# Sums of states as the moving side, and gate weights turned on VectorE, in the head of an attention and expert kernel

## The chip, the cores and the metric

The kernel runs on one core of one Trainium2 chip. The metric is the device time of one execution in microseconds (us). Three executions of the kernel before took 437.92, 438.87 and 439.55 us; the median is 438.87. The profiled execution has a span of 434.3 us, and all times within the program are counted from the start of that span.

## What is computed

The first block is a cross attention between tokens x and states, for each of 8 batches and 8 heads, with 512 tokens, 32 states and a head width of 64:

```python
scores = scale * np.matmul(x, state.transpose(0, 1, 3, 2))
a = softmax(scores)
xread = np.matmul(a, state)          # tokens read states
a2 = softmax(scale * np.matmul(state, x.transpose(0, 1, 3, 2)))
sread = np.matmul(a2, x)             # states read tokens
rows = concatenate([xread, sread])   # (8 * 544 rows, 512 wide)
```

The second block routes each of these 4352 rows to one of 8 experts:

```python
logits = rows @ w_gate                       # 512 x 8
e = argmax(logits);  gate = softmax(logits)[e]
out = gate * (maximum(rows @ w1[e], 0) @ w2[e])   # w1: 512 x 1024, w2: 1024 x 512
```

All of it is float32.

## The kernel before, in words

The kernel takes the batches one after the other. For most batches nearly all token rows go to one and the same expert, so a batch is computed with the expert that most of its rows choose, and the rows that chose otherwise are treated apart at the end. Because a token row is a weighted mean of states, the kernel never forms it: it multiplies the states of the batch with w1 (a product called G, from PSUM tiles pG), and then G with the turned attention weights (aT) to get the hidden layer (PSUM tiles ph, SBUF tiles hT), and last with w2 (py, pX and other PSUM tiles).

**The order** of all instructions is written out by hand: each engine's wrapper `InOrder` (line 48, hence the L48 in nearly every row of the profile) keeps the program order on its engine. A wait at the head of an engine's queue holds all that is behind it. The scheduler adds the semaphores between engines.

**The head.** Batch 0 has a start of its own, `begin` (line 443). Before it, the program issues the first loads: `load_states(0, sp, act)` (line 111) puts the 32 state rows into partitions 0 to 31 of `st2[0]` with one DMA on SyncE's queue, and the same rows with the two halves of each head exchanged into partitions 32 to 63 with two DMAs on ScalarE's queue. Then ScalarE's queue issues the gate weights `wg4` (line 112), in which partition p holds rows 4p to 4p+3 of w_gate, and SyncE's queue the two halves of x of batch 0 (line 113). VectorE and GpSimd prepare constants meanwhile; VectorE ends this with a memset of `gst` (line 187), a tile of which only 8 of each 32 columns are written later.

`begin` first makes a guess of batch 0's expert, so that w1 can be fetched before attention is computed: the column sums of the states times w_gate. `keep_warm(n)` (line 543) issues n matmuls of the identity with itself into a PSUM tile that nobody reads (`idle`); they keep TensorE busy. A float32 matmul shows as two records in the profile. The sums are four matmuls (PSUM tile `pss`), whose stationary side is a strided piece of the states of 32 x 128 and whose moving side is one column of ones; VectorE copies them to `sums` (128 x 4), and four more matmuls (`prg`) multiply them with the columns of wg4. `most` (line 435) finds the number of the largest of 8 on VectorE (`c_m`, `c_cc`, `eb`), and `expert_of` (line 549) reads it into a register of SyncE, after which SyncE issues the two halves of that expert's w1, then x and states of batch 1, the gate weights in another order, w2, and batch 2.

In the meantime VectorE turns the states in blocks of 32 x 32 (`turn_states`, tile `stT`, of which ScalarE copies the lower partitions to the upper ones, and GpSimd makes the copies `stG` that pG uses) and then the first half of x (`turn_x`, tile `xt`). TensorE runs six warming matmuls and then the scores of batch 0 (PSUM tile `pc`), 64 matmuls of 32 x 32 x 128; the first half of them needs stT and the first half of x. Behind pc, VectorE and ScalarE compute the softmax in pieces (`sx`, `mx`, `sm`) and turn it to aT (tile `aTe`), and TensorE multiplies G with it.

Of the kernel before, what the change touches and what calls it, by code (L numbers as in the profile page):

```python
# [9 lines left out]
FP32 = mybir.dt.float32  # L10
# [3 lines left out]
ALU = mybir.AluOpType  # L14
AX = mybir.AxisListType
# [5 lines left out]
def kernel(  # L21
# [32 lines left out]
    pe, dve, act, gp, sp = (InOrder(e) for e in (nc.tensor, nc.vector, nc.scalar, nc.gpsimd, nc.sync))  # L54
# [4 lines left out]
    E = moe_w_gate.shape[1]  # L59
# [7 lines left out]
    NDC = DM // 128  # L67
# [21 lines left out]
    att = tc.alloc_tile_pool(name="att", bufs=1)  # L89
# [3 lines left out]
    def load_x(b, q):  # L93
        x_nat[b] = att.tile([128, H, NC, D], FP32, tag="x", bufs=3, name="x_nat")
        for h in (slice(0, 4), slice(4, 8)):
            q.dma_start(out=x_nat[b][:, h].rearrange("p h c d -> p h (c d)"),
                        in_=x[b, h].rearrange("h (p c) d -> p h (c d)", c=NC))

    st2 = {}

    def load_states(b, q0, q1):

        rows = state[b].rearrange("h n d -> n h d")
        to = st2[b] = att.tile([64, H, D], FP32, tag="st", bufs=3, name="st2")
        q0.dma_start(out=to[0:32], in_=rows)
        for u in range(2):
            q1.dma_start(out=to[32:64, :, ts(u, 32)], in_=rows[:, :, ts(1 - u, 32)])

    wg = const.tile([128, NDC, E], FP32)
    wg4 = att.tile([128, NDC, E], FP32, name="wg4")  # L110
    load_states(0, sp, act)
    act.dma_start(out=wg4[:], in_=moe_w_gate.rearrange("(p c) e -> p c e", c=NDC))
    load_x(0, sp)
    warm = const.tile([128, 1], FP32)
    dve.memset(warm[:], 0.0)
    act.activation(warm[:], warm[:], AF.Exp)
# [2 lines left out]
    ident = const.tile([128, 128], FP32)  # L119
# [12 lines left out]
    ones_f = att.tile([128, 1], FP32, name="ones_f")  # L132
# [51 lines left out]


    gst = att.tile([128, B, 2, 32], FP32, name="gst")
    dve.memset(gst[:], 0.0)


    blank = ffn.tile([128, XW], I32, tag="y", bufs=YB, name="blank")  # L190
    gp.memset(blank[:], 0)
    gp.memset(blank[:, DM + 1:DM + 2], FAR)

    soft, rows_of = {}, {}
    G = hT = None

    def bank(name):
        return ps_p.tile([128, 512], FP32, tag="p", name=name)
# [3 lines left out]
    def turn_x(b, xt, k):  # L202

        dve.transpose(xt[k][:].rearrange("p h c u t -> p (h c u t)"),
                      x_nat[b][:, ts(k, 4)].rearrange("p h c d -> p (h c d)"))

    def turn_states(b, copy):

        stT[b] = att.tile([128, H, 2, NS], FP32, tag="stT", bufs=2, name="stT")
        to = stT[b][:].rearrange("p h u n -> p (h u n)")  # L210
        dve.transpose(to[0:64], st2[b][:].rearrange("p h d -> p (h d)"))
        copy(to[64:128], to[0:64])
        for g in range(2):
            gp.tensor_copy(out=stG[ts(g, 64), b], in_=stT[b][:].rearrange("p (q g) u n -> p g u q n", g=2)[ts(g, 64), g, 0])
# [61 lines left out]
    def new_xt(b):  # L276

        return [(att, ffn)[b % 2].tile([128, 4, NC, 2, 32], FP32, tag=("xt0", "xt1", "Sa", "Sb")[2 * (b % 2) + k], name="xt")
                for k in range(2)]

    def new_sx():
        return att.tile([128, 4, NB, NS], FP32, tag="sx", bufs=2, name="sx")
# [152 lines left out]
    def most(b, pr):  # L435
        n = pr.shape[0]
        m = att.tile([n, 1], FP32, tag="c_m", bufs=2, name="c_m")
        dve.tensor_reduce(m[:], pr, AX.X, ALU.max)
        cc = att.tile([n, E], FP32, tag="c_cc", bufs=2, name="c_cc")
        dve.scalar_tensor_tensor(cc[:], pr, m[:], io8[0:n], ALU.is_ge, ALU.mult)  # L440
        dve.tensor_reduce(eb[0:n, b:b + 1], cc[:], AX.X, ALU.max)

    def begin():

        nonlocal G, hT

        keep_warm(3)
        ps = bank("pss")[:, 0:4]
        for q in range(4):
            pe.matmul(ps[:, q:q + 1], lhsT=st2[0][0:32].rearrange("n h d -> n (h d)").rearrange("n (p c) -> n c p", c=4)[:, q, :],  # L450
                      rhs=ones_f[0:32], start=True, stop=True, skip_group_check=True)
        sums = att.tile([128, 4], FP32, name="sums")
        dve.tensor_copy(out=sums[:], in_=ps)
        pr = bank("prg")[0:1, 0:E]
        for q in range(4):
            pe.matmul(pr, lhsT=sums[:, q:q + 1], rhs=wg4[:, q, :], start=(q == 0), stop=(q == 3), skip_group_check=True)
        most(0, pr)
        keep_warm(6)
        turn_states(0, act.copy)
        xt, sx = new_xt(0), new_sx()  # L460
        turn_x(0, xt, 0)
        e = expert_of(eb, 0)
        at_once(w1_parts(0, e, 2))
        load_x(1, sp)
        load_states(1, sp, sp)
        sp.dma_start(out=wg[:], in_=moe_w_gate.rearrange("(c p) e -> p c e", p=128))
        at_once(w2_parts(0, e))
        fetch_batch(2)
        turn_x(0, xt, 1)
        pc = new_pc()  # L470
        for qs in ((0, 1), (2, 3)):
            for g in range(2):
                scores(0, xt, pc, g, qs)
        one, two, half = slice(0, 1), slice(1, 2), slice(2, 4)
        soft[0] = (sx,)
        G, hT = new_G(), new_hT()
        turn_scores(pc, sx, 0)
        less_max(sx, one, dve)
        exponential(sx, one)
        states_w1(G, w1s[0], stG[:, 0], (0,), cut=2)  # L480
        turn_scores(pc, sx, 1)
        over_sum(sx, one, dve)
        turn_read(0, one)
        less_max(sx, two, dve)
        exponential(sx, two)
        keep_warm(5)
        near, far = range(NFC // 2), range(NFC // 2, NFC)
        up(G, aT[0], hT, one, fs=near)
        states_w1(G, w1s[0], stG[:, 0], (1,))
        turn_scores(pc, sx, 2)  # L490
        turn_scores(pc, sx, 3)
        over_sum(sx, two, dve)
        turn_read(0, two)
        up(G, aT[0], hT, two, fs=near)
        less_max(sx, half, dve)
        exponential(sx, half)
        over_sum(sx, half, dve)
        turn_read(0, half)
        for r in range(NR):
            sp.dma_start(out=ss_dram[ts(r, 128)], in_=blank[:])  # L500
        up(G, aT[0], hT, one, fs=far)
        up(G, aT[0], hT, two, fs=far)
        nm = write_max(pc)
        xt, sx = new_xt(1), new_sx()
        for k in range(2):
            turn_x(1, xt, k)
        turn_states(1, gp.tensor_copy)
        first_e = att.tile([1, 1], FP32, name="first_e")
        dve.tensor_copy(out=first_e[:], in_=eb[0:1, 0:1])

        def beside():
            nonlocal nm, pc
            soft[0] += write_weights(pc, nm)
            states_gates(0)
            yield
            states_gates(1)
            pc = new_pc()
            scores(1, xt, pc, 0)
            yield

            pr = bank("pre")[:, 0:1]
            pe.matmul(pr, lhsT=ones_f[0:1].to_broadcast([1, 128]), rhs=first_e[:], start=True, stop=True)
            scores(1, xt, pc, 1)
            dve.tensor_copy(out=eb[:, 0:1], in_=pr)
            for i in range(4):
                turn_scores(pc, sx, i)
            less_max(sx, ALL, dve)
            nm = write_max(pc)
            yield
            exps, gates = logits_x(0)  # L530
            turn_write(0)
            exponential(sx, ALL)
            soft[1] = (sx,) + write_weights(pc, nm)
            exps()
            early.append(stages(2))
            next(early[0])
            gates()
            over_sum(sx, ALL, dve)
            turn_read(1)
            yield  # L540
        up(G, aT[0], hT, half, beside())

    def keep_warm(n):

        idle = bank("idle")
        for _ in range(n):
            pe.matmul(idle[:, 0:128], lhsT=ident[:], rhs=ident[:], start=True, stop=True, skip_group_check=True)

    def expert_of(table, i, engines=(SP,)):
        _, (e,) = nc.values_load_multi_w_load_instructions(  # L550
            table[0:1, i:i + 1], engines=list(engines), min_val=0, max_val=E - 1,
            skip_runtime_bounds_check_because="the table holds experts' numbers")
        return e
# [16 lines left out]
    def at_once(parts):  # L570
        for p in parts:
            p()
# [616 lines left out]
    with tc.If(number(rest_i, B * S + NG) > 0, label="rest") as cmp:  # L1189
# [4 lines left out]
        with tc.If(number(left_i, B * S) > 0):  # L1194
# [18 lines left out]
            with tc.For_i(0, n_pairs, 1):  # L1213
# [14 lines left out]
                e = expert_of(px, 0)  # L1228
# [5 lines left out]
                             in_=at_dram[ds(bb, 1)].rearrange("o p s -> p (o s)"))  # L1234
# [61 lines left out]
```

## Time and profile before

| | busy us | share of the span |
|---|---|---|
| TensorE matmul (PE) | 425.9 | 98% |
| TensorE weight load (PEld) | 289.6 | 67% |
| VectorE (DVE) | 220.3 | 51% |
| GpSimd (POOL) | 153.3 | 35% |
| ScalarE (ACT) | 129.0 | 30% |

In the first 16 us the engines stand thus:

| start us | what |
|---|---|
| 0.84, 1.29, 1.79 | ScalarE's queue issues the two pieces of states and the gate weights |
| 0.87, 1.33 | SyncE's queue issues the state rows and the two halves of x |
| 1.47 to 3.12 | first warming matmuls |
| 3.34 to 5.33 | sums of the states |
| 6.29 to 6.64 | prg |
| 6.57 to 9.50 | second warming matmuls |
| 9.43 to 12.33 | scores pc |
| 13.27 to 14.48 | first half of pG |
| 16.14 | first products ph |

A row of the profile names the tile that is written and those that are read (out<-in), the shapes, the count, and in brackets the idle time of the engine just before and what ended it. PE is a matmul, PEld a load of its stationary side; an engine's name with a q is its queue, as where a DMA is issued. Busy time of an engine that works beside another costs nothing; what counts is the chain of waits, in which each piece of time is put down to the work that the next piece waited for.

### The profile page before, as it was taken

What the parts mean: (1) busy time and instruction counts of PE and PEld (TensorE: products, weight loads), DVE (VectorE), ACT (ScalarE), POOL (GpSimd) and SP (SyncE); (2) the same over time, 40 slices, a digit from 0 to 9 for tenths busy, and PEclk for the clock granted to TensorE, in tenths of its full rate; (3) what the DMA queues carried; (4) which work ended last, traced back from release to release, by engine and by line L of the source; (5) the groups of instructions that cost most, each with busy time, mean ns of one, the idle gap of its engine ahead of it and who ended that gap; (6) DMA issues with size and microseconds to landing.
All of it is one profiled execution on the core that took longest, in us unless ns stands there. A gap on an engine that the chain in (4) does not pass through costs nothing.

```text
span 434.3 us, 10177 instructions
## 1 busy us (share of the span) xinstructions
PE 425.9 (98%) x3927; PEld 289.6 (67%) x3927; DVE 220.3 (51%) x473; ACT 129.0 (30%) x297; POOL 153.3 (35%) x143
## 2 busy tenths in 40 slices
PE   7899999999999999999999999999999999999996
PEld 7676555555545558686668667776867685768665
DVE  5668966587686547434424251624442370527142
ACT  1455134552451532213221241013240242015100
POOL 2010231233222513473327424634335253644231
PEclk9999999999999999999999999999999999999999
DMA  5991559753685444999999699689947998875312
GB/s 144 342 344 41 188 191 307 225 211 122 206 307 171 157 172 129 293 341 390 384 386 395 220 342 384 250 279 397 386 151 239 406 379 281 312 260 200 97 36 73
DMA packets 64513, 110.04 MB, mean 253 GB/s; under 512 B 12943, under 2 KB 22415, under 8 KB 64464
## 3 DMA queue, kind: packets, MB, share of 16 engines
q1 hardware_dynamic: 60240, 99.99, 66.7%
q0 software_dynamic: 2240, 7.08, 4.3%
q10 hardware_dynamic: 1984, 2.31, 1.5%
q8 instruction: 32, 0.52, 0.5%
q14 instruction: 17, 0.14, 0.1%
HBM read 94.15 MB, written 14.95 MB: 251 GB/s over the span
## 4 chain that ended last, share of the span: by engine, by line
PE 95%; DVE 2%; DMA 1%; ACT 0%; issue 0%; ACTq 0%; POOL 0%; DVEq 0%
PE ph L48 23%; PE py L48 13%; PE pX L48 10%; PE pD L48 8%; PE pY L48 5%; PE pZ L48 5%; PE pgh L48 5%; PE pgy L48 5%; PE pW L48 5%; PE pc L48 4%; PE pG L48 3%; PE pw L48 2%; PE pt L48 2%; PE pE L48 2%; DMA wg<-in_moe_w_gate_dram 1%; PE pl L48 1%
## 5 line engine op out<-in xcount | busy, mean ns | idle before, releaser
L48 PE MATMUL py<-w2t,hT 128*128 128x512 f32 x128 | 59.1, 604 | 0.0
L48 DVE TENSOR_TENSOR hT<-ph,hT 128x512 f32<-128x512 f32 x50 | 34.6, 692 | 40.7 <-PE ph L48 40.7
L48 POOL TENSOR_TENSOR Ta<-w2t,Ta 128x1024 f32<-128x1024 f32 x12 | 30.6, 2549 | 46.6 <-PE pY L48 19.9
L48 PE MATMUL pX<-w2t,hT 128*128 128x256 f32 x192 | 43.7, 381 | 0.0
L48 PEld LDWEIGHTS py<-w2t,hT 128*128 128x128 f32 x128 | 23.0, 189 | 26.3 <-issue 25.3
L48 PEld LDWEIGHTS pX<-w2t,hT 128*128 128x128 f32 x192 | 36.2, 190 | 6.4 <-issue 1.7
L48 ACT ACTIVATE hT<-ph 128x512 f32<-128x512 f32 (+2 forms) x50 | 22.7, 462 | 40.1 <-PE ph L48 40.1
L48 PE MATMUL ph<-aTl,G 128*128 128x256 f32 (+1 forms) x112 | 33.8, 444 | 0.0
L48 DVE SCALAR_TENSOR_TENSOR yh<-pY,gw,yh 128x256 f32<-128x256 f32 x22 | 9.2, 478 | 44.3 <-PE pY L48 37.7
L48 PE MATMUL ph<-aTe,G 128*128 128x128 f32 (+2 forms) x128 | 30.4, 388 | 0.5 <-DVE aTe L48 0.4
L48 ACT ACTIVATE yh<-pX,gw 128x256 f32<-128x256 f32 x34 | 13.7, 474 | 52.6 <-PE pX L48 52.6
L48 POOL DMA_DIRECT2D out_dram<-yh x23 | 16.8, 730 | 34.3 <-DVE yh L48 17.7
L48 ACT ACTIVATE hT<-hT 128x512 f32<-128x512 f32 x30 | 18.9, 630 | 30.7 <-DVE hT L48 30.7
L48 PEld LDWEIGHTS ph<-aTl,G 128*128 128x128 f32 x112 | 20.6, 190 | 9.6 <-issue 7.7
L48 POOL TENSOR_TENSOR sx<-sx,mx 128x1024 f32<-128x1024 f32 x6 | 11.5, 1913 | 38.4 <-DVE mx L48 38.4
L48 PEld LDWEIGHTS ph<-aTe,G 128*128 128x128 f32 x128 | 18.8, 191 | 9.3 <-issue 6.5
L48 ACT COPY G<-pG 128x512 f32<-128x512 f32 (+1 forms) x34 | 17.1, 568 | 24.3 <-PE pG L48 24.3
L48 ACT COPY hT<-ph 128x512 f32<-128x512 f32 x10 | 5.9, 586 | 55.1 <-issue 43.1
L48 PE MATMUL pY<-Ta,Sa 128*128 128x256 f32 x96 | 22.2, 384 | 0.0
L48 PE MATMUL pZ<-Tb,Sb 128*128 128x256 f32 x96 | 22.1, 383 | 0.0
L48 PEld LDWEIGHTS pY<-Ta,Sa 128*128 128x128 f32 x96 | 17.8, 190 | 6.4 <-issue 3.4
L48 POOL TENSOR_TENSOR Tb<-w2t 128x1024 f32<-128x1024 f32 x6 | 14.2, 2370 | 22.2 <-issue 22.2
(184 smaller groups left out, 737.5 us busy)
## 6 DMA issues: line engine op xcount, KB each, us to landing
s<-in_moe_w_dram SPq DMA_DIRECT2D x192, 256.0 KB, 5.9
w2t<-in_moe_w_dram SPq DMA_DIRECT2D x32, 512.0 KB, 6.8
w1t<-in_moe_w_dram SPq DMA_DIRECT2D x28, 512.0 KB, 6.8
x_nat<-in_x_dram SPq DMA_DIRECT2D x16, 512.0 KB, 5.3
out_dram<-yh POOLq DMA_DIRECT2D x23, 256.0 KB, 5.2
at_dram<-aTl SPq DMA_DIRECT2D x6, 512.0 KB, 6.4
w1t<-in_moe_w_dram SPq DMA_DIRECT2D x2, 1024.0 KB, 5.1
out_dram<-y ACTq DMA_DIRECT2D x8, 256.0 KB, 5.6
```

The source lines that it names most:

```text
L48: ins = getattr(self.engine, name)(*args, **kw)
```

## The change

The guess of batch 0's expert is computed in another way. The states become the moving side of four matmuls against a 32 x 32 block of ones: the matmul of column group q gives the sums of columns 128q to 128q+127, repeated in 32 partitions. The gate weights are loaded first on ScalarE's queue, into a tile padded with zeros to 32 columns for each of the four rows of a partition, and VectorE turns that tile in blocks of 32 x 32, so that partition 32q+e holds the 128 weights of expert e for group q. VectorE multiplies the sums with them and adds over the 128 elements. Four matmuls against columns of the identity add the four groups and bring the eight logits into one partition. The purpose is a guess that needs less TensorE work before it and does not wait for the gate weights.

Besides, one of the first warming matmuls is dropped, the memset of gst moves from VectorE to GpSimd, and the first half of x is turned ahead of the states rather than behind them.

```diff
-    wg4 = att.tile([128, NDC, E], FP32, name="wg4")
+    wg4 = att.tile([128, NDC, 32], FP32, name="wg4")
+    act.dma_start(out=wg4[:, :, 0:E], in_=moe_w_gate.rearrange("(p c) e -> p c e", c=NDC))
     load_states(0, sp, act)
-    act.dma_start(out=wg4[:], in_=moe_w_gate.rearrange("(p c) e -> p c e", c=NDC))
     load_x(0, sp)
+    dve.memset(wg4[:, :, E:], 0.0)
...
     gst = att.tile([128, B, 2, 32], FP32, name="gst")
-    dve.memset(gst[:], 0.0)
...
     gp.memset(blank[:, DM + 1:DM + 2], FAR)
+    gp.memset(gst[:], 0.0)
...
-        keep_warm(3)
-        ps = bank("pss")[:, 0:4]
+        keep_warm(2)
+        ps = bank("pss")[:, 0:128]
         for q in range(4):
-            pe.matmul(ps[:, q:q + 1], lhsT=st2[0][0:32].rearrange("n h d -> n (h d)").rearrange("n (p c) -> n c p", c=4)[:, q, :],
-                      rhs=ones_f[0:32], start=True, stop=True, skip_group_check=True)
-        sums = att.tile([128, 4], FP32, name="sums")
-        dve.tensor_copy(out=sums[:], in_=ps)
+            pe.matmul(ps[ts(q, 32)], lhsT=ones_f[0:32].to_broadcast([32, 32]), rhs=st2[0][0:32, ts(q, 2), :],
+                      start=True, stop=True, skip_group_check=True)
+        wgT = att.tile([128, NDC, 32], FP32, name="wgT")
+        dve.transpose(wgT[:].rearrange("p c t -> p (c t)"), wg4[:].rearrange("p c e -> p (c e)"))
+        prod = att.tile([128, 32, NDC], FP32, name="prod")
+        dve.tensor_tensor(prod[:], ps.rearrange("p (t c) -> p t c", c=NDC), wgT[:].rearrange("p c t -> p t c"), ALU.mult)
+        sums = att.tile([128, 1], FP32, name="sums")
+        dve.tensor_reduce(sums[:], prod[:], AX.XY, ALU.add)
         pr = bank("prg")[0:1, 0:E]
         for q in range(4):
-            pe.matmul(pr, lhsT=sums[:, q:q + 1], rhs=wg4[:, q, :], start=(q == 0), stop=(q == 3), skip_group_check=True)
+            pe.matmul(pr, lhsT=sums[:], rhs=ident[:, ds(32 * q, E)], start=(q == 0), stop=(q == 3), skip_group_check=True)
         most(0, pr)
         keep_warm(6)
-        turn_states(0, act.copy)
         xt, sx = new_xt(0), new_sx()
         turn_x(0, xt, 0)
+        turn_states(0, act.copy)
```

## The prediction

> **What bounds the kernel now.** I read the page first: its row of slices says that TensorE is the engine to watch from start to end.
>
> ```profile
> PE   7899999999999999999999999999999999999996
> PE 95%; DVE 2%; DMA 1%; ACT 0%; issue 0%; ACTq 0%; POOL 0%; DVEq 0%
> ```
>
> The first line is TensorE's busy share in slices of 10.9 us, the second the chain that ended last, by engine. TensorE is gapless but for the first two slices, so the body can't be shortened by this edit: only what ends before TensorE's unbroken run counts, and each microsecond saved there moves everything behind it. So I went to the chain of waits of the first 60 us:
>
> ```profile
> 1.79 4.37 DMA wg<-in_moe_w_gate_dram
> 6.16 0.14 issue
> 6.29 0.35 PE prg L48 x8
> 6.64 2.86 PE idle L48 x12
> 9.50 2.83 PE pc L48 x120
> ...
> 16.14 2.02 PE ph L48 x16
> ```
>
> Columns: start, length, what. The first guess of the expert (prg) waits for the gate weights until 6.16, though the sums of states it needs are older, as the timeline of the head shows:
>
> ```profile
> 3.34 1.99 PE L48 MATMUL pss<-ones_f,st 32*128 32x1 f32 x8 [0.23 <-DMA st<-in_state_dram]
> 5.37 0.16 DVE L48 COPY sums<-pss 128x4 f32<-128x4 f32 x1 [1.61 <-PE pss L48]
> 7.19 0.15 DVE L48 TENSOR_REDUCE eb<-c_cc 1x1 int32<-1x8 f32 x1
> 7.30 0.70 DVE L48 STREAM_TRANSPOSE stT<-st 64x512 f32<-64x512 f32 x1
> 7.94 2.32 DVE L48 STREAM_TRANSPOSE xt<-x_nat 128x1024 f32<-128x1024 f32 x2
> 8.04 0.62 ACT L48 COPY stT<-stT 64x512 f32<-64x512 f32 x1 [4.25 <-DVE stT L48]
> 8.07 0.97 SPq L48 DMA_DIRECT2D w1t<-in_moe_w_dram  x2
> 13.27 1.21 PE L48 MATMUL pG<-w1t,stG 64*32 64x512 f32 x16 [0.95 <-DMA w1t<-in_moe_w_dram]
> ```
>
> The guess eb is complete at 7.34 (call it E). Two paths leave it and meet at the first up products (ph, 16.14). One: SyncE reads eb, issues w1 at 8.07, its first half lands by 13.27, pG and the copies of G follow; ph's weight load waits for G until 16.11. Two: the turned states and x, the scores pc (9.43 to 12.33), the softmax on VectorE, the turned weights aTe, for which ph's matmul waits until 16.14. They end 0.03 us apart, so **both** must shrink.
>
> **What the Trainium skill says.** "TensorE: Matmul & The Clock Gate", Part 1: the array runs at half rate until a free-running window of about 3.4 us has been busy. The trace agrees: the 12 warming records at 6.57 take 2.93 us (244 ns each), ten at 14.41 take 1.38 (138 ns). Inside pc the rate changes too: its weight loads are 172 ns in the median up to about 10.9 and 104 ns later, 4.6 us after prg began. The same page, Part 3: matmuls in distinct column groups run side by side. Agreed: the 16 records of pl, 128 columns in four groups, take 0.65 us in all. "VectorE: DVE Perf Modes", on the errata: a float32 tensor_tensor takes (N+151)/0.96 ns, 291 ns at N = 128; a 128x128 one (ge) measures 291. "DMA: Bandwidth & Descriptors", Queues, rings and completion order: each DMA engine alternates between queues with work, packet by packet. This fits the gate weights: third on ScalarE's queue, beside 1 MB of x, they need 4.4 us for 16 KB, while the two state pieces ahead need 2.8 in the median.
>
> **The change, part by part.** Times from the span's start.
>
> Gate weights first: issued at 0.84 in place of 1.79. Landing: 2.8 us, as the pieces that were first, gives 3.64; 4.4 would give 5.2. I take 3.64, since x isn't flowing before 2. Turning them (wgT) is a 128x128 transpose, 0.31 by the row of lg, done by 3.95.
>
> State rows: still first on SyncE, landed by 3.34. The sums: four matmuls, two records each, 128 columns in four groups: half of pl's 0.65, doubled for the cold clock, 0.65; were they to run one after the other, 8 x 244 ns = 1.95, what they cost now. I take 0.65: end 4.0 in place of 5.33.
>
> VectorE: the product with wgT, 0.29 by the row of ge; the sum over 128 elements, 0.29 by the row of eg_f (128x128, 286 ns); with 0.05 us from TensorE, done at 4.63. This replaces a copy of 0.16. A strided operand may make the product dearer; twice the row adds 0.3.
>
> prg: the same eight records, now on the identity: 0.12 to start (as aTe at 16.01 to ph at 16.14) and 0.35: 5.1. From its end to E it was 0.70: **E = 5.8, 1.54 earlier**.
>
> Path one: 0.73 from E to the w1 issue, 5.1 to land, 2.84 from pG to ph's weight load: 5.8 + 0.73 + 5.1 + 0.1 + 2.84 = **14.6, against 16.11**. x is off the DMA engines by 6.6, so the earlier w1 finds them free.
>
> Path two: the x half comes first. It was issued at 1.33 and needs 4.6 us (the shortest of the x landings): 5.93, so it starts at 5.95 rather than 5.8. One of two transposes in 2.32 takes 1.16, states 0.66 to 0.70, ScalarE's copy 0.62, hand-overs 0.2: pc at **8.6 in place of 9.43**. The warming matmuls behind prg would end at 5.1 + 2.86 = 8.0, so the new order makes TensorE wait 0.6 us: the states with their copy are last, where before the warming hid them. The second x half (issued 1.8, 5.6 us at worst: 7.4) is turned from 7.8 to 9.0, ahead of pc's second half. pc's state pieces in partitions 32 to 63 are now behind the gate weights; the last may need wg's 4.4 or somewhat more after 1.79, 6.2 to 6.9. The transpose behind it needs it at 7.1: hidden by the x transpose.
>
> pc's length depends on the clock. Before, it ran 1.5 us cold and 1.4 warm. A warm 64 records take 1.07 (at 29.71), so the warm part held 82 records and the cold part 46, 30 per us. From 8.6: all warm 2.14, end 10.75; cold until the same 10.9, 69 records and then 59 warm in 1.0, end 11.9; a change near 10, midway, gives about 11.4. I take 11.4, 0.9 earlier than 12.33, and VectorE's 3.8 us from there to ph: **15.2**.
>
> The later path sets the end: 15.2 against 16.14. With the clock's phase open between 14.6 and 15.7, **the gain is 0.4 to 1.55 us, I take 1.1**, a little over the middle, since before's own clock change could fall later than in this one profile.
>
> At nothing: one warming matmul less (it ends near 2.6, TensorE waits for states until 3.34); the pad memset on VectorE (96 elements, between 0.06 for warm and 0.48 for gst, in its 0.77 us of waiting for colf); the gst memset moved to GpSimd (about 0.52, as blank's; GpSimd is idle from 2.92 to 8.07). The pad lies between DMA-written columns. The two state pieces, interleaved in the same partitions too, were issued back to back with no wait, so I expect none here. No bytes are added. GpSimd's stG copies come 0.4 us later than w1's shift would have them, at 8.9, and w1 lands at 11.6.
>
> **Rivals.**
> *B, all warm.* The earlier prg lets the clock change before pc. Path two ends at 10.75 + 3.8 = 14.55, path one at 14.6: gain 1.5, 437.3. For: four microseconds between prg and pc. Against: the phase is free.
> *C, the gap keeps the array cold (slower).* The 0.6 us hole before pc, and the shorter busy stretch ahead of it, spoil the window; a busy one then ends only after 12. pc cold: 128/30 = 4.25, end 12.85; ph 12.85 + 3.8 = 16.65, and pG at double 1.21 pushes G by another 0.3 to 1: +0.5 to +1.3, 439.7. For: pc was already half cold. Against: the head before had holes as well[...].
> *D, the wait moves.* The pad memset waits for the gate DMA, or that lands with x at 5.2. With the set-up on VectorE (1.6 us) behind 3.64, wgT comes at 5.2 to 5.5, E at 6.9: 0.4 gained, 438.4. For: nothing in before shows a memset beside a DMA in one tile. Against: the state pieces.
>
> **How the numbers follow.** A 0.55, B 0.2, C 0.13, D 0.12. A gives 438.87 - 1.1 = 437.8. Three times of before spread over 1.6 us, so a case's time is uncertain by some 0.7. The range takes in B with that, down to 436.4, and most of C, up to 440.0. Half a per cent is 2.2 us, 436.7 and 441.1, more than the working gives: a third of B and a sixth of A could pass the lower mark (0.16), and 0.02 for a gain not seen here; for the upper, a third of C and some unseen cost, 0.08.
>
> **What would show it.** pss in 0.5 to 0.8 us; wgT complete before the product starts; eb near 5.8 and w1 issued near 6.5; the x half starting at 5.9 to 6.0; a hole of about 0.6 us before pc; weight loads in pc changing from 172 to 104 ns near 10; ph near 15.1; behind it the same TensorE rows. Wrong would be: pss one after the other, VectorE's set-up starting at 3.6, states landing after 7.1, pc cold throughout, or a gap further down that the head's shift has opened.

## The result and the profile after

The changed kernel took 436.40 us in the median of six executions (434.70 to 436.62) against 439.45 for the kernel before (six, 437.92 to 439.77). The ratio is 0.9927, with a 95% interval of 0.9905 to 0.9949: **3.2 us gained, between 2.2 and 4.2**. Forecast were 1.1 us.

The profile does not show that gain where the prediction looked for it. The profiled execution of after has a span of 434.8 us, half a microsecond *more* than the 434.3 of before. In its chain of waits the first products ph start later, not earlier:

```profile
2.19 5.64 DMA st<-in_state_dram
7.83 0.03 issue
7.86 0.05 DVEq L48
7.91 0.05 issue
7.96 0.71 DVE stT L48
8.67 0.04 issue
8.71 0.64 PE pc L48 x4
9.35 0.01 issue
9.36 3.51 PE pc L48 x118
...
16.69 2.02 PE ph L48 x16
```

Columns: start, length, what. The gate weights are off this chain; a piece of states that lands at 7.83 has taken their place. Behind it pc needs 3.5 us and ph starts at 16.69, against 16.14 before. The timeline of the same head shows that the guess itself went as planned, and in this execution better:

```profile
0.84 0.65 ACTq L48 DMA_DIRECT2D wg<-in_moe_w_gate_dram  x1
2.97 0.65 PE L48 MATMUL pss<-st,ones_f 32*32 32x128 f32 x8 [0.29 <-POOL blank L48]
3.68 0.37 DVE L48 TENSOR_TENSOR prod<-pss,wgT 128x128 f32<-128x128 f32 x1 [0.17 <-PE pss L48]
4.08 0.29 DVE L48 TENSOR_REDUCE sums<-prod 128x1 f32<-128x128 f32 x1
5.31 0.15 DVE L48 TENSOR_REDUCE eb<-c_cc 1x1 int32<-1x8 f32 x1
6.10 1.25 DVE L48 STREAM_TRANSPOSE xt<-x_nat 128x1024 f32<-128x1024 f32 x1 [0.64 <-DMA x_nat<-in_x_dram]
7.96 0.70 DVE L48 STREAM_TRANSPOSE stT<-st 64x512 f32<-64x512 f32 x1 [0.61 <-DMA st<-in_state_dram]
8.71 4.14 PE L48 MATMUL pc<-xt,stT 32*32 32x128 f32 x128 [1.09 <-DVE stT L48]
12.79 1.22 PE L48 MATMUL pG<-w1t,stG 64*32 64x512 f32 x16
```

The sums take 0.65 us rather than 1.99, and eb is complete at 5.46 rather than 7.34. Then the row of stT waits for its DMA, and pc takes 4.14 us: it runs cold throughout, that is, at the lower of TensorE's two clocks, since the trace has the full clock from 13.1 on.

So how can the device time fall? **It is longer than the span**, which runs from the first to the last recorded instruction. The profiled execution of before took 438.42 us at a span of 434.3: 4.1 us lie outside. That of after took 436.56 at 434.8: 1.8. What the DMA engines moved between 434 and 440 us, before:

```profile
DMA packets 1, 0.01 MB, mean 1 GB/s; under 512 B 0, under 2 KB 0, under 8 KB 0
q14 instruction: 1, 0.01, 0.6%
```

and after, in the same stretch:

```profile
DMA packets 0, 0.00 MB, mean 0 GB/s; under 512 B 0, under 2 KB 0, under 8 KB 0
```

In before one packet of instructions (8 KB, from 436.3 to 436.9) is fetched behind the last recorded instruction. In after the last such packet runs at 431.1, within the span. The last record of the trace, one of the granted clock, ends 4.4 us behind the span's end in before and 2.0 us in after: the difference lies at the end of the program, not ahead of the first instruction. The theory that I then tested: about 2.3 us of the gain are this fetch, and the head brings the rest. Its rival: the head brings all, and the one profile of before was a lucky execution.

### The profile page after: what moved, and what is told of

It reads as the page before. It is cut to its first block, busy times and chain, and to the rows that moved or that the text cites. A ratio compares the mean times of both kernels' runs of the same rounds, so it can differ in the third digit from the quotient of the medians.

```text
span 434.8 us, 10177 instructions
## 1 busy us (share of the span) xinstructions
PE 425.4 (98%) x3925; PEld 287.9 (66%) x3925; DVE 220.6 (51%) x475; ACT 128.9 (30%) x297; POOL 153.7 (35%) x144
## 4 chain that ended last, share of the span: by engine, by line
PE 94%; DVE 2%; DMA 1%; ACT 0%; issue 0%; ACTq 0%; POOL 0%; DVEq 0%
PE ph L48 23%; PE py L48 13%; PE pX L48 10%; PE pD L48 8%; PE pY L48 5%; PE pZ L48 5%; PE pgy L48 5%; PE pgh L48 5%; PE pW L48 5%; PE pc L48 4%; PE pG L48 3%; PE pw L48 2%; PE pt L48 2%; PE pE L48 2%; DMA st<-in_state_dram 1%; PE pl L48 1%
```

## The experiments

Each result gives device time and span of every execution; "outside" is the median of their difference. Ratios are to runs of the kernel before in the same series, and a gain in microseconds is what the ratio lacks to 1, times the median of those runs (439.45 for after; 438.88, 439.32, 438.96 and 439.00 in the four series of experiments, in each of which all kernels ran on one chip).

| kernel | device us | span us | outside us | ratio, 95% interval |
|---|---|---|---|---|
| after | 436.40 | 434.6 | 1.8 | 0.9927 (0.9905 to 0.9949) |
| before, again | 438.95 | 434.9 | 4.1 | 1.0005 (0.9997 to 1.0014) |
| before, three more on VectorE | 438.91 | 434.7 | 4.0 | 0.9992 (0.9982 to 1.0002) |
| before, gst on GpSimd | 436.45 | 434.7 | 1.8 | 0.9942 (0.9924 to 0.9959) |
| before, one more on GpSimd | 436.65 | 434.9 | 1.8 | 0.9944 (0.9928 to 0.9960) |
| after, gst on VectorE | 438.33 | 434.2 | 4.1 | 0.9977 (0.9968 to 0.9987) |
| before, gates first | 437.62 | 433.6 | 4.1 | 0.9968 (0.9955 to 0.9980) |
| after, states first | 436.88 | 435.1 | 1.8 | 0.9957 (0.9941 to 0.9972) |
| after, compact gates | 434.91 | 433.2 | 1.8 | 0.9905 (0.9887 to 0.9923) |
| after, nine warming | 435.76 | 434.0 | 1.8 | 0.9915 (0.9898 to 0.9932) |
| compact, states first | 434.92 | 433.1 | 1.8 | 0.9908 (0.9892 to 0.9924) |
| gates first, gst on GpSimd | 435.33 | 433.6 | 1.8 | 0.9917 (0.9901 to 0.9933) |
| compact, seven warming | 434.83 | 433.1 | 1.8 | 0.9905 (0.9887 to 0.9922) |
| compact, gst on VectorE | 437.13 | 432.9 | 4.1 | 0.9960 (0.9945 to 0.9975) |
| before, sixteen more on GpSimd | 436.17 | 434.4 | 1.8 | 0.9943 (0.9930 to 0.9957) |
| nine warming, gst on VectorE | 437.80 | 433.7 | 4.1 | 0.9977 (0.9969 to 0.9984) |

The span leaves the end of the program out and so allows executions to be pooled that differ only there. Mean spans, with the standard error: before 434.93 (0.06, 92 executions); the changed head, gst on either engine, 434.14 (0.14, 28); with the compact load 433.21 (0.15, 13); with nine warming matmuls 433.82 (0.09, 25); before with the gates first 433.45 (0.14, 13). The means of before in the four series are 434.80, 435.10, 434.79 and 434.96, so differences of 0.3 us between kernels of different series say little.

### What lies outside the span

**The kernel before, unchanged.**

> The kernel before, unchanged, for the span of each of its executions beside its device time. Tail theory: of the 3.05 us between the medians, some 2.3 lie behind the last recorded instruction, where an 8 KB instruction fetch at 436.3 follows the span of before and none follows the span of after; so device time minus span is about 4.1 us in every execution here (after: 1.8), and the spans lie at 434 to 435.5. Head theory: the whole gain is a shorter head, the one profile of before was a lucky one; device time minus span is about 1.8 in most executions and the spans lie near 437.5.

Outside were 3.97 to 4.30 us in all 13 executions, spans 433.9 to 435.6. The profile of before was no lucky one; the rival falls.

**More instructions on VectorE.**

```diff
     dve.memset(gst[:], 0.0)
+    pad = const.tile([128, 3], FP32)
+    for k in range(3):
+        dve.memset(pad[:, k:k + 1], 0.0)
```

> The kernel before with three more memsets of one column each on VectorE behind that of gst, where VectorE idles for 1.6 us; its VectorE program then has as many instructions as that of after. Tail theory: if VectorE's stream is the one whose last block is fetched behind the end, device time falls to some 436.5 to 437 with spans as in the kernel before, and device time minus span to about 1.8. Head theory: no change at all, 439.4, since the head is the same.

Nothing changed: 438.91, 4.0 outside. The three instructions moved another packet, from 181 to 170 us, and left the late one 2.1 us behind the span's end, where it is in before. So the stream that is fetched at the end is not VectorE's, which was my first guess.

**The memset of gst on GpSimd, and nothing else of the change.**

```diff
-    dve.memset(gst[:], 0.0)
...
     gp.memset(blank[:, DM + 1:DM + 2], FAR)
+    gp.memset(gst[:], 0.0)
```

> The kernel before with one edit of the change alone: the memset of gst on GpSimd behind those of blank, not on VectorE. In the head this hides (0.52 us while GpSimd idles), so the spans should stay at 434.8 in the median. Tail theory, now for GpSimd's stream (three more VectorE instructions left the difference at 4.0): one more GpSimd instruction moves the last block's fetch into the span, device time minus span falls from 4.1 to about 1.8 and device time to 436.6. Rival: the tail depends on another engine's stream or on the total; then nothing changes, 438.9.

436.45, a gain of 2.5 us (1.8 to 3.3), at spans like those of before (434.8 against 435.1 in the mean, within the noise). One moved memset does most of what the whole change does.

**The whole change but for that move.**

```diff
+    dve.memset(gst[:], 0.0)
...
-    gp.memset(gst[:], 0.0)
```

> The changed kernel with the memset of gst back on VectorE, behind the set-up: the GpSimd program then has as many instructions as before. Tail theory for GpSimd: device time minus span goes back to 4.1 and device time to 438.8 to 439.3, so that nothing is left of the gain of the whole change. Besides, the turn of the gate weights starts 0.5 us later, at 3.76, and the guess by 0.3. Rival: the tail is not GpSimd's; device time grows by 0.3 at most, 436.7.

The 4.1 us outside are back, in all of 22 executions (3.99 to 4.51). Device time is 438.33: 1.0 us (0.6 to 1.4) faster than before, where I had written 438.8 or more. This is the gain of the rest of the change, which the parts of the head have to explain.

**One tiny memset on GpSimd.**

```diff
     gp.memset(blank[:, DM + 1:DM + 2], FAR)
+    pad = const.tile([128, 1], FP32)
+    gp.memset(pad[:], 0.0)
```

> The kernel before, gst still cleared on VectorE, with one more memset of a single column on GpSimd behind blank (0.1 us, while GpSimd idles). If it is the number of GpSimd's instructions that decides whether its last block is fetched inside the span, device time minus span is 1.8 and device time 436.6 with spans as before, the same as when the memset of gst was moved. If the move itself brought it (VectorE free half a microsecond sooner, or a longer memset on GpSimd), this changes nothing: 439.0, difference 4.1.

436.65, 1.8 outside, a gain of 2.5 us (1.8 to 3.2) from an instruction that computes nothing used. gst stayed on VectorE, so neither VectorE's time nor a longer memset is the cause: one more instruction in GpSimd's stream is enough. The stretch from 434 to 440 us in this kernel's DMA view:

```profile
DMA packets 0, 0.00 MB, mean 0 GB/s; under 512 B 0, under 2 KB 0, under 8 KB 0
```

and in the changed kernel with gst on VectorE:

```profile
DMA packets 1, 0.01 MB, mean 1 GB/s; under 512 B 0, under 2 KB 0, under 8 KB 0
q14 instruction: 1, 0.01, 0.5%
```

**Sixteen instead of one.**

```diff
-    pad = const.tile([128, 1], FP32)
-    gp.memset(pad[:], 0.0)
+    pad = const.tile([128, 16], FP32)
+    for k in range(16):
+        gp.memset(pad[:, k:k + 1], 0.0)
```

> The kernel before with sixteen more memsets of one column on GpSimd behind blank in place of one (1.6 us while it idles). If the last block's fetch starts at a fixed instruction of GpSimd's stream, sixteen more only bring it further forward within the span: 1.8 outside, 436.6. If what matters is alignment to something smaller, or only an odd count, 4.1 outside return and the time is 439.0.

436.17, 1.8 outside, a gain of 2.5 us (1.9 to 3.1): it is neither parity nor a fine alignment. But the last packet did not come further forward, as the expectation had it: it begins at 430.66, and in the kernel with only one instruction more on GpSimd (the memset of gst) at 430.65. Its place does not follow GpSimd's count.

All kernels of the study fall into two groups in this way: with GpSimd's count as before, a packet at 434.8 to 437.9, behind the last instruction, and 4.0 to 4.1 us outside in the median; with more, the last packet at 429.0 to 431.2 and 1.8 outside. One profile, that of nine warming matmuls with gst on VectorE, has two packets behind the end, at 435.5 and 437.9:

```profile
DMA packets 2, 0.02 MB, mean 3 GB/s; under 512 B 0, under 2 KB 0, under 8 KB 0
q14 instruction: 2, 0.02, 1.1%
```

That execution has 4.75 us outside, the most of all.

What the extra instruction does to the packets is more than a shift. Every profile with more GpSimd instructions has a packet at 349 to 352 that no profile of the other group has (with sixteen more it comes at 326.3), and another 3.7 us ahead of the span's end; the one behind the end is gone. The packets that move with GpSimd's count are an earlier one, from 127.7 to 95.1 with sixteen more, both times near GpSimd's 70th recorded instruction, and the one at 351. **That the count of GpSimd's instructions decides about the 2.3 us is shown by adding and removing one; that the late packet is what the end waits for is argued from the traces**, in which the two always go together, and how one packet more in mid-program spares the one behind the end stays open.

### The parts of the head

**The gate weights first, in the kernel before.**

```diff
+    act.dma_start(out=wg4[:], in_=moe_w_gate.rearrange("(p c) e -> p c e", c=NDC))
     load_states(0, sp, act)
-    act.dma_start(out=wg4[:], in_=moe_w_gate.rearrange("(p c) e -> p c e", c=NDC))
```

> The kernel before with one edit of the change alone: the gate weights issued ahead of the two state pieces on ScalarE's queue. The guess no longer waits for the gates but for the old sums: eb near 6.4 in place of 7.34. The state pieces then land near 7.8 and the first x half is turned behind them, so the scores start near 9.9 in place of 9.43: the span is 0.3 to 0.5 us longer if the landing of the states is what binds, 0.5 to 1 us shorter if the guess is. Device time minus span is 4.1 in the tail theory (same instruction counts as before).

A gain of 1.4 us (0.9 to 2.0), all in the span. The guess binds, not the landing of the states: they were ready at 6.58, not 7.8. This load goes into a tile without gaps and is issued in 0.40 us, the new, padded one in 0.65; what the gaps cost is measured next. In the profile eb is complete at 6.38, and pc and ph are early:

```profile
6.58 0.70 DVE L48 STREAM_TRANSPOSE stT<-st 64x512 f32<-64x512 f32 x1 [0.20 <-DMA st<-in_state_dram]
8.46 2.73 PE L48 MATMUL pc<-xt,stT 32*32 32x128 f32 x128
15.03 1.69 PE L48 MATMUL ph<-aTe,G 128*128 128x128 f32 x13 [0.25 <-DVE aTe L48]
```

So one moved line, with the old sums, brings as much as the whole changed head: by the ratios 1.4 us (0.9 to 2.0) against 1.0 (0.6 to 1.4). Its mean span is 0.7 us shorter in the pool, but 0.4 when each is set against before in its own series, at a standard error near 0.3: a lead of the one line is not shown.

**The compact gate load.** In the changed kernel the padded tile is filled from a small one:

```diff
+    wg_c = att.tile([128, NDC, E], FP32, name="wg_c")
-    act.dma_start(out=wg4[:, :, 0:E], in_=...)
+    act.dma_start(out=wg_c[:], in_=...)
...
+        dve.tensor_copy(out=wg4[:, :, 0:E], in_=wg_c[:])
         dve.transpose(wgT[:].rearrange("p c t -> p (c t)"), ...)
```

> The changed kernel with the gate weights loaded without gaps (128 pieces of 128 bytes, as before) and copied on VectorE to the padded tile, in place of a load straight into it (512 pieces of 32 bytes: the profile of after counts 386 more packets). If the small pieces hold up the state pieces behind them, the gate issue falls from 0.65 to 0.40 us, the states land near 6.6 rather than 7.8, the scores start near 8.7 rather than 9.36, and the span is 0.3 to 0.7 us shorter (device time 435.7 to 436.1). If what holds them is x on the other queue, they land as late as in after and nothing is gained; the copy costs 0.15 us at most.

434.91, spans 1.5 us shorter than those of after in the median, more than expected, but from six executions each, and the two ratios' intervals overlap. ScalarE's queue up to 17 us in after, then in this kernel (packets, MB, share of the engines):

```profile
q10 hardware_dynamic: 1072, 0.08, 4.2%
```

```profile
q10 hardware_dynamic: 688, 0.08, 3.1%
```

The bytes are the same, the packets 384 more: four pieces of 32 bytes for each of 128 partitions instead of one of 128. The timeline of the compact kernel:

```profile
0.83 0.40 ACTq L48 DMA_DIRECT2D wg_c<-in_moe_w_gate_dram  x1
3.13 0.28 DVE L48 COPY wg<-wg_c 128x32 f32<-128x32 f32 x1
7.21 0.66 DVE L48 STREAM_TRANSPOSE stT<-st 64x512 f32<-64x512 f32 x1
8.57 1.99 PE L48 MATMUL pc<-xt,stT 32*32 32x128 f32 x124 [0.16 <-ACT stT L48]
11.68 1.22 PE L48 MATMUL pG<-w1t,stG 64*32 64x512 f32 x16 [1.11 <-DMA w1t<-in_moe_w_dram]
14.40 2.02 PE L48 MATMUL ph<-aTe,G 128*128 128x128 f32 x16 [0.20 <-DVE aTe L48]
```

stT no longer waits for its DMA, and pc, in this execution warm (at full clock from 8.1 on), is short. pG waits for w1 again, and ph starts at 14.40, when both G and aTe have just come. The copy takes 0.28 us on VectorE. To measure the head alone I gave this kernel the end of before as well (gst on VectorE):

> The changed kernel with the compact gate load and gst cleared on VectorE: GpSimd's count is that of before, so what lies outside the span is 4.1 us on both sides and the ratio shows the head alone. If the small pieces of the padded load cost the change some 1.5 us of its head, as the medians of spans suggest, the ratio is about 0.994 (2.5 us gained), clear of the 0.9977 of the same kernel with the padded load. If that difference was chance of the clock's phase in six executions, the ratio is 0.9965 to 0.998.

0.9960, 1.8 us gained (1.1 to 2.4), against 1.0 (0.6 to 1.4) with the padded load: less than the 2.5 foretold, and the intervals still touch. The pooled spans tell more: 434.14 against 433.21, 0.9 us apart at standard errors of 0.15, and 0.9 as well when each is set against before in its own series. **The padded load costs about 0.9 us** (some 0.5 to 1.3), not 1.5.

**States first, in the changed kernel.**

```diff
-        turn_x(0, xt, 0)
         turn_states(0, act.copy)
+        turn_x(0, xt, 0)
```

> The changed kernel with the old order of turns: states, then the first half of x. In the profile of after the states' last piece lands at 7.83 and the x half is ready at 6.09. If the order pays as intended, VectorE now waits for the states at 7.96 with x behind it, the scores start at about 9.9 rather than 9.36, and the span grows by 0.5 us (less if the scores then run warm). If the order costs nothing or harms (the wait for the states' copy), the span is the same or shorter by up to 0.3 us. Device time minus span stays 1.8 in the tail theory.

435.1 in the span, against 434.6 for after: the expected 0.5, though the intervals of the two ratios overlap. The mean span, 435.24 (standard error 0.25), lies 1.1 above that of the 28 pooled executions of the changed head. In the profile VectorE waits for the states until 7.55, with the x half behind it, and pc starts at 9.44. With the compact load the same edit gives:

> The compact gate load with the old order of turns, states ahead of the x half. With the states landing at 6.6 and x ready at 6.0 the two orders should tie: the states are turned from 6.6 to 7.25 and copied beside the x half, scores from about 8.5 (8.57 in the profile of the compact load). Median within 0.3 us of 434.9. If turning x first pays in general, this is 0.5 us slower; if the copy of the states on the path is what that order costs, 0.5 us faster.

434.92 against 434.91: a tie. Turning x first repairs a delay that the padded load had made; without the delay it brings nothing measurable.

**Nine warming matmuls, in the changed kernel.**

```diff
-        keep_warm(6)
+        keep_warm(9)
```

> The changed kernel with nine warming matmuls behind the guess in place of six, which reach from 4.7 to 9.1 when cold and so fill the hole before the scores. If the hole is what leaves the array cold (scores 4.1 us long in after, full clock at 13.1 in its profile), full clock comes between 7.8 and 11.2, the scores shrink to 2.1 to 3.3 us, and the median span falls by about 0.8 us, device time to 435.6, with a narrower or shifted spread. If the hole has no part in it, full clock stays near 13 and the time at 436.4, or grows by up to 0.2 where the extra matmuls are in the way.

435.76, spans 434.0 rather than 434.6, near what was expected, but not resolved: the intervals overlap. In its profile full clock comes at 11.4 (13.1 in after) and pc takes 2.88 us rather than 4.14. Again with the end of before, beside the kernel that gave 0.9977:

> The changed kernel with gst on VectorE, as in the run that gave 0.9977, and nine warming matmuls in place of six: the hole before the scores filled, the end of the program as before on both sides. If the hole keeps the array cold in many executions, the ratio falls to about 0.996 to 0.9965 (0.6 to 0.8 us gained by the warming) and the spans spread less than the 432.9 to 435.4 there. If the hole has no part in it, it stays at 0.9977.

0.9977: nothing gained in device time. The spans spread less, as foretold (433.3 to 434.5 over 19, against 432.9 to 435.4 over 22), and pooled they are 0.3 us shorter, about twice the standard error; against before in their own series 0.2 and 0.3, which is not resolved. So the hole costs at most a few tenths in the mean. Two things may limit what a fill can bring: in this profile pc starts at 9.45, when the last warming matmul is done, but ScalarE's copy of the states ends at 9.45 too; and in the profile without the fill the full clock came at 8.5 despite the hole.

**Two edits of one line each, and one more warming matmul on top of the compact load.**

> The kernel before with two one-line edits of the change and nothing of the new sums: gate weights first on ScalarE's queue, gst cleared on GpSimd. If the two add up: 437.6 less 2.3 is 435.3, spans at 433.6 and a difference of 1.8, so about 1 us faster than the whole change. If the new sums are needed for the gain in the span, it is no better than 436.4.

435.33, as the sum of the two foretold. The gate weights first and one memset on GpSimd, with the old sums, give a median 1.1 us below that of the whole change, but by the ratios only 0.4 us, and their intervals overlap. The two edits do as much as the whole change; that they do more is not shown.

> The compact gate load with seven warming matmuls behind the guess in place of six; cold they end near 8.3 rather than 7.8, ahead of the scores at 8.57. If what is left of a hole there still lets the clock fall behind in some executions, the spread narrows and the median falls by up to 0.3 us from 434.9; if not, it stays within 0.2.

434.83, spans 432.3 to 433.7: the same as the compact kernel within what these runs tell. The compact kernels are the fastest of the study: about 0.95% (0.8 to 1.1) faster than the kernel before, 1.5 us below the change in their medians and 1.0 by the ratios (two of after's six executions lie well below its median).

## Why the prediction was wrong, step by step

**The step that failed** is under "at nothing": "the gst memset moved to GpSimd (about 0.52, as blank's; GpSimd is idle from 2.92 to 8.07)". The time of the memset is hidden, as said. But it is one more instruction in GpSimd's stream, and with it the packet of instructions behind the end is gone: 2.5 us (1.8 to 3.3) by itself, where the prediction had put nothing. The rest of the 3.2 is the head. Behind this lies the first paragraph's "only what ends before TensorE's unbroken run counts": the device time also has an end behind the last instruction. The sign could be read beforehand: 438.42 against a span of 434.3, and an instruction packet at 436.3. What no view of before could tell is that 1.8 is what remains, and which engine to give the instruction to. The Trainium skill ("Runtime: NRT & Kernel Launch", Instruction fetch mechanics) says that the engines fetch their instructions block by block while they run and that the cost of a block's end is mostly hidden; a packet behind the last recorded instruction goes here with 2.3 us more outside the span (4.1 against 1.8), so at the program's end it was not hidden.

**The head's sum was right in total** (1.1 against 1.0, interval 0.6 to 1.4, with gst on VectorE; 0.8 in pooled spans) **and wrong in its parts**, so that the total is in part luck: errors of both signs cancelled.

- *The sums, 0.65 us*: 0.65. The product was 0.37, not 0.29; the reduction 0.29.
- *E = 5.8*: 5.46 in the profile of after, 6.1 to 6.3 in those of the others with the padded load. The landing of the gate weights, which the turn waits for in those, varies: from before 3.2 to 4.1, around the 3.64 assumed. In those four profiles the guess still waits for the gate weights, which the change was to avoid.
- *The last state piece at 6.2 to 6.9, hidden*: 7.83 in after, and so on the path. "No bytes are added" was true and beside the point: 384 more packets were. The compact load, with which VectorE had them by 6.31 in the one profile that shows it (states first), gives about 0.9 us of span back.
- *pc at 8.6*: four of its records at 8.71, the others at 9.36. The hole before pc was 1.1 us instead of 0.6, and another 0.5 us behind the first four records, which need only partitions 0 to 63 of the turned states, not ScalarE's copy.
- *pc ending near 11.4*: 12.85 in the profile, rival C's figure to the digit, with full clock at 13.1. But of after's six spans two are 432.9 and 433.3 and four 434.6 to 434.9; the two may be rival B's case. They have no profile of their own, so that is argued. But that case does occur in this head: in the profile of the changed kernel with gst on VectorE the full clock comes at 8.5, and 124 records of pc take 1.99 us.
- *Path one, 14.6*: w1 came in time, but pG stands behind pc in TensorE's queue and started at 12.79, not 11.7. The prediction had not carried pc's end into this path.
- *Rival D*: nothing of it. The pad memset ran at 0.93, beside the gate DMA.

**The range**, 436.4 to 440.0, ended where the median fell, since no case knew of the end of the program.

## What to carry to other kernels

Compare the device time with the span before you cost an edit: if more lies outside than the program's end explains, see whether an instruction packet is fetched behind the last instruction, and try an idle instruction more on one engine after the other before anything larger (here GpSimd's counted and VectorE's did not; ScalarE, SyncE and TensorE were not tried). A DMA is priced by its pieces as well as its bytes: the padded destination cut 16 KB into 512 pieces instead of 128, and what waited behind it in the same queue paid. When several edits come as one, run the cheapest alone; here two lines did as much as the change that they came with.

## What was not expected of the hardware

- One GpSimd instruction of 0.1 us, added while the engine was idle, shortened the device time by 2.5 us; three on VectorE did nothing. Sixteen did what one did; whether many more would bring the late packet back was not tried.
- A load of 16 KB in 512 pieces of 32 bytes was issued in 0.65 us, against 0.40 us in 128 pieces of 128; the state pieces behind it landed at 7.83 in one profile, against 6.58 with the same order and the compact form.
- In the profile of the changed kernel with gst on VectorE, ph starts at 15.23, 0.9 us ahead of before, but the span is 434.6, longer than before's 434.3. Of the 1.2 us lost in between, 0.9 arise in one place, where TensorE stands still in the middle of a later pc and the profile shows nothing that it waits for:

```profile
68.54 0.43 PE L48 MATMUL pc<-xt,stT 32*32 32x128 f32 x10 [0.93 <-issue]
```

A packet of instructions on another queue (q8) ends at 67.2 in that execution, 0.4 us before the stop begins; whether this is the cause stays open.
